# A streaming x + alpha * fx: chunks of two sizes, and three stores on ScalarE's DMA queue

## The chip, the cores and the metric

The kernel runs on one core of one Trainium2 chip. The metric is the device time of one execution in microseconds (us); lower is better. Times before: the median of 7 runs is 152.57 us, from 152.4 to 153.15.

## The reference

```python
B, S, D = 512, 32, 640
# x, fx: (B, S, D) bf16; alpha: (1,) bf16

def reference(x, fx, alpha):
    return x + alpha * fx
```

Each element is read once from x and once from fx, and written once. Each tensor has 10,485,760 elements, 20.97 MB.

## The kernel before

Each tensor is seen as 128 partitions of 81,920 consecutive elements. These are cut into five chunks of 16,384 columns (`CHUNK`), so one transfer of a chunk is 128 rows of 32 KB, 4.19 MB.

alpha is fetched once with a small DMA on ScalarE's queue and spread over the 128 partitions by a matmul with ones (`alpha_to_lanes`, L17 to L27). It is then a per-partition scalar in `a_f`.

For each chunk k there are four steps:

- `load_x(k)` (L57, DMA issued at L59) into a tile of the pool `xs`, which has four buffers
- `load_f(k)` (L61, DMA at L63) into a tile of the pool `fs`, which has two buffers
- `compute(k)` (L65, instruction at L69): one VectorE instruction, f * a_f + x, written in place over the x tile. `compute(4, 2)` does it in two halves
- `store(k)` (L78, DMA at L80) from the x tile to the output. Chunk 4 is stored in two halves

All loads and stores are issued by SyncE (`nc.sync`), thus on one DMA queue, in the order in which L85 to L105 name them, since the schedule is manual. Where an instruction needs something that isn't there yet, the tile framework lets it wait, and what stands behind it on the same engine waits too. The waits that matter here:

- `compute(k)` waits for both its loads
- `store(k)` waits for its compute
- `load_f(k)` waits for `compute(k-2)`, which read the same buffer of `fs`
- `load_x(4)` waits until `store(0)` has landed, since `xs` has four buffers

In the queue the transfers then stand as x0, f0, x1, f1, x2, f2, store 0, x3, f3, store 1, x4, f4, store 2, store 3, and the two halves of store 4.

Of the kernel before, what the change touches and what calls it, by code (L numbers as in the profile page):

```python
# [1 line left out]

# [4 lines left out]

ACT = mybir.ActivationFunctionType
ALU = mybir.AluOpType
F32 = mybir.dt.float32  # L10
BF16 = mybir.dt.bfloat16

CHUNK = 16384


def alpha_to_lanes(nc, consts, psum, alpha, eng):

    P = nc.NUM_PARTITIONS
    a_1 = consts.tile([1, 1], alpha.dtype, name="a_1")
    eng.dma_start(out=a_1[:], in_=alpha[None, :])  # L20
    ones = consts.tile([1, P], alpha.dtype, name="ones")
    nc.vector.memset(ones[:], 1.0)  # L22
    a_ps = psum.tile([P, 1], F32, name="a_ps")
    nc.tensor.matmul(a_ps[:], ones[:], a_1[:], start=True, stop=True)  # L24
    a_f = consts.tile([P, 1], F32, name="a_f")
    nc.vector.tensor_copy(out=a_f[:], in_=a_ps[:])  # L26
    return a_f  # L27


@with_exitstack  # L30
def kernel(
    ctx: ExitStack,
    tc: tile.TileContext,
    x: bass.AP,
    fx: bass.AP,
    alpha: bass.AP,
    out: bass.AP,
):
    nc = tc.nc
    P = nc.NUM_PARTITIONS  # L40
    xv = x.flatten_outer_dims().rearrange("(p n) d -> p (n d)", p=P)
    fxv = fx.flatten_outer_dims().rearrange("(p n) d -> p (n d)", p=P)
    ov = out.flatten_outer_dims().rearrange("(p n) d -> p (n d)", p=P)
    F = xv.shape[1]
    K = F // CHUNK
    assert K * CHUNK == F and K == 5

    consts = ctx.enter_context(tc.tile_pool(name="consts", bufs=1))
    psum = ctx.enter_context(tc.tile_pool(name="psum", bufs=1, space=bass.MemoryType.PSUM))
    xs = ctx.enter_context(tc.tile_pool(name="xs", bufs=4))  # L50
    fs = ctx.enter_context(tc.tile_pool(name="fs", bufs=2))
    ctx.enter_context(tc.manual_schedule())

    a_f = alpha_to_lanes(nc, consts, psum, alpha, nc.scalar)
    xt, ft = {}, {}

    def load_x(k):  # L57
        xt[k] = xs.tile([P, CHUNK], x.dtype, tag="x", name="x_t")
        nc.sync.dma_start(out=xt[k][:], in_=xv[:, bass.ts(k, CHUNK)])  # L59

    def load_f(k):  # L61
        ft[k] = fs.tile([P, CHUNK], fx.dtype, tag="f", name="f_t")
        nc.sync.dma_start(out=ft[k][:], in_=fxv[:, bass.ts(k, CHUNK)])  # L63

    def compute(k, parts=1):  # L65
        n = CHUNK // parts
        for j in range(parts):
            s = bass.ts(j, n)
            nc.vector.scalar_tensor_tensor(  # L69
                out=xt[k][:, s],  # L70
                in0=ft[k][:, s],
                scalar=a_f[:],
                in1=xt[k][:, s],
                op0=ALU.mult,
                op1=ALU.add,
            )

    def store(k, j=0, parts=1):  # L78
        n = CHUNK // parts
        nc.sync.dma_start(  # L80
            out=ov[:, k * CHUNK + j * n : k * CHUNK + (j + 1) * n],
            in_=xt[k][:, bass.ts(j, n)],
        )

    load_x(0)  # L85
    load_f(0)
    load_x(1)
    load_f(1)
    load_x(2)
    compute(0)  # L90
    load_f(2)
    store(0)
    load_x(3)
    compute(1)
    load_f(3)
    store(1)
    load_x(4)
    compute(2)
    load_f(4)
    store(2)  # L100
    compute(3)
    store(3)
    compute(4, 2)
    store(4, 0, 2)
    store(4, 1, 2)  # L105


# [1 line left out]
_INS = ['x', 'fx', 'alpha']  # L109
_OUTS = [((512, 32, 640), 'bfloat16')]  # L110


# [23 lines left out]
```

## Time and profile before

| what | value |
|---|---|
| median of 7 runs | 152.57 us |
| the profiled execution | 153.07 us |
| its span, from the first to the last instruction | 151.3 us |
| bytes read, written | 41.94 MB, 20.97 MB |
| one compute of 16,384 columns, of 8,192 | 17.29 us, 8.75 us |
| last compute begins, second half ends | 121.56 us, 138.97 us |
| first DMA issue | 0.73 us |

A profile is of one execution. Its engine rows cut the span in 40 equal slices and give the busy share of each slice in tenths. The DMA row is the mean over the core's 16 DMA engines, on which the rows of one transfer are spread, 8 rows on each. DVE is VectorE, SP is SyncE, ACT is ScalarE; SPq is SyncE's sequencer, which issues the DMAs and waits for semaphores. A wait there delays only what is issued behind it; transfers that are already in the queue go on.

### The profile page before, as it was taken

Reading aid. Unit: us, or ns where it says so; the run is one execution under the profiler, and the core shown is the slowest. Engines: PE = TensorE matmul, PEld = TensorE weight load, DVE = VectorE, ACT = ScalarE, POOL = GpSimd, SP = SyncE. Lnnn points to the kernel's source line nnn. Section 1 sums busy time; section 2 is a strip of 40 time slices with the busy share of each in tenths; the row PEclk is TensorE's granted clock in tenths of the full one; section 3 lists DMA queues with packets and bytes.
Section 4 is the critical chain, followed back from the end, with each engine's and each line's share of the span. In section 5 each row is a group of like instructions: output and inputs, shape, how many; then the busy total and the mean of one; then the engine's idle time right before and its main releaser. Section 6 shows DMA issues by size and latency. Waiting matters only on the chain.

```text
span 151.3 us, 85 instructions
## 1 busy us (share of the span) xinstructions
PE 0.2 (0%) x1; PEld 0.1 (0%) x1; DVE 86.9 (57%) x8; POOL 0.2 (0%) x4
## 2 busy tenths in 40 slices
PE   0000000000000000000000000000000000000000
PEld 0000000000000000000000000000000000000000
DVE  0000009999689997599990007999800089997000
POOL 0000000000000000000000000000000000000000
DMA  6999999999999999999999999999999999999993
GB/s 199 442 442 442 416 416 416 433 451 450 442 442 416 416 416 416 390 442 416 416 416 442 450 433 416 425 451 425 416 433 450 433 433 425 433 425 403 425 429 156
DMA packets 2306, 62.92 MB, mean 416 GB/s; under 512 B 258, under 2 KB 258, under 8 KB 258
## 3 DMA queue, kind: packets, MB, share of 16 engines
q1 hardware_dynamic: 2304, 62.92, 97.6%
q10 hardware_dynamic: 2, 0.00, 0.0%
HBM read 41.94 MB, written 20.97 MB: 416 GB/s over the span
## 4 chain that ended last, share of the span: by engine, by line
DMA 56%; DVE 29%; DVEq 6%; issue 0%; SPq 0%
DMA f_t<-in_fx_dram 56%; DVE x_t L69 29%; DVEq L131 6%; SPq L59 0%; DVEq L69 0%
## 5 line engine op out<-in xcount | busy, mean ns | idle before, releaser
L69 DVE SCALAR_TENSOR_TENSOR x_t<-f_t,a_f,x_t 128x16384 bf16<-128x16384 bf16 (+1 forms) x6 | 86.6, 14439 | 50.1 <-DMA f_t<-in_fx_dram 50.1
L26 DVE COPY a_f<-a_ps 128x1 f32<-128x1 f32 x1 | 0.2, 158 | 1.2 <-PE a_ps L24 1.2
L22 DVE MEMSET ones<- 1x128 bf16 x1 | 0.2, 165 | 0.8 <-PEq L120 0.8
L24 PE MATMUL a_ps<-a,ones 1*128 1x1 bf16 x1 | 0.2, 158 | 1.9 <-DMA a<-in_alpha_dram 1.9
L120 POOL MEMSET const-bfloat16-1.0<- 128x1 bf16 x1 | 0.1, 101 | 0.0
L120 POOL MEMSET const-uint8-127<- 128x1 uint8 x1 | 0.1, 101 | 0.0
L24 PEld LDWEIGHTS <-ones 1*128 1x128 bf16 x1 | 0.1, 100 | 1.0 <-DVE ones L22 1.0
L120 POOL MEMSET const-float32-0.0<- 128x1 f32 x1 | 0.1, 98 | 0.2 <-issue 0.2
L120 POOL MEMSET const-float32-1.0<- 128x1 f32 x1 | 0.1, 98 | 0.0
## 6 DMA issues: line engine op xcount, KB each, us to landing
x_t<-in_x_dram SPq DMA_DIRECT2D x5, 4096.0 KB, 34.9
f_t<-in_fx_dram SPq DMA_DIRECT2D x5, 4096.0 KB, 32.2
out_dram<-x_t SPq DMA_DIRECT2D x4, 4096.0 KB, 36.6
out_dram<-x_t SPq DMA_DIRECT2D x2, 2048.0 KB, 15.2
a<-in_alpha_dram ACTq DMA_DIRECT2D x1, 0.0 KB
```

What stands on the lines that cost most here:

```text
L22: nc.vector.memset(ones[:], 1.0)
L24: nc.tensor.matmul(a_ps[:], ones[:], a_1[:], start=True, stop=True)
L26: nc.vector.tensor_copy(out=a_f[:], in_=a_ps[:])
L69: nc.vector.scalar_tensor_tensor(out=xt[k][:, s], in0=ft[k][:, s], scalar=a_f[:], in1=xt[k][:, s], op0=ALU.mult, op1=ALU.add,)
L120: nc = _bacc.Bacc("TRN2", target_bir_lowering=False, num_devices=1)
L131: with _tile.TileContext(nc) as tc:
```

## The change

The chunks get two sizes: four of 8,192 columns (2.10 MB a transfer), then three of 16,384. The pools keep their number of buffers, and each buffer keeps room for 16,384 columns. `store` takes the engine that issues it. The stores of chunks 0, 1 and 2 are issued by ScalarE, those of chunks 3 to 6 by SyncE. In the loop `store(k - 3, ...)` is on ScalarE for k = 4 and 5, and on SyncE for k = 6. The last chunk is computed and stored in two halves, as before.

SyncE's order becomes x0, f0, x1, f1, x2, f2, x3, f3, x4, f4, x5, f5, store 3, x6, f6, store 4, store 5, and the two halves of store 6. ScalarE's order, behind alpha's DMA, is store 0, store 1, store 2. The waits on buffers are now `load_f(k)` on `compute(k-2)`, and x4, x5, x6 on the landing of stores 0, 1 and 2.

```diff
-CHUNK = 16384
+SIZES = [8192, 8192, 8192, 8192, 16384, 16384, 16384]
+STARTS = [sum(SIZES[:k]) for k in range(len(SIZES))]
+SLOT = max(SIZES)
...
+    def cols(k):
+        return slice(STARTS[k], STARTS[k] + SIZES[k])
+
     def load_x(k):
-        xt[k] = xs.tile([P, CHUNK], x.dtype, tag="x", name="x_t")
-        nc.sync.dma_start(out=xt[k][:], in_=xv[:, bass.ts(k, CHUNK)])
+        xt[k] = xs.tile([P, SLOT], x.dtype, tag="x", name="x_t")
+        nc.sync.dma_start(out=xt[k][:, : SIZES[k]], in_=xv[:, cols(k)])
...
-    def store(k, j=0, parts=1):
-        n = CHUNK // parts
-        nc.sync.dma_start(
-            out=ov[:, k * CHUNK + j * n : k * CHUNK + (j + 1) * n],
-            in_=xt[k][:, bass.ts(j, n)],
-        )
+    def store(k, eng=nc.sync):
+        eng.dma_start(out=ov[:, cols(k)], in_=xt[k][:, : SIZES[k]])
...
     load_x(2)
     compute(0)
     load_f(2)
-    store(0)
+    store(0, nc.scalar)
     load_x(3)
-    compute(1)
-    load_f(3)
-    store(1)
-    load_x(4)
-    compute(2)
-    load_f(4)
-    store(2)
-    compute(3)
-    store(3)
-    compute(4, 2)
-    store(4, 0, 2)
-    store(4, 1, 2)
+    for k in range(4, len(SIZES)):
+        compute(k - 3)
+        load_f(k - 1)
+        store(k - 3, nc.scalar if k < 6 else nc.sync)
+        load_x(k)
+    compute(4)
+    load_f(6)
+    store(4)
+    compute(5)
+    store(5)
+    n = SIZES[6] // 2
+    for s in (slice(0, n), slice(n, 2 * n)):
+        nc.vector.scalar_tensor_tensor(
+            out=xt[6][:, s], in0=ft[6][:, s], scalar=a_f[:], in1=xt[6][:, s], op0=ALU.mult, op1=ALU.add
+        )
+        nc.sync.dma_start(out=ov[:, STARTS[6] + s.start : STARTS[6] + s.stop], in_=xt[6][:, s])
```

`load_f` changes as `load_x` does, and `compute(k)` works on the first `SIZES[k]` columns of its tiles with one instruction.

More of the change, by code (lines that the diff above doesn't have):

```diff
@@ L44 @@
     F = xv.shape[1]
-    K = F // CHUNK
-    assert K * CHUNK == F and K == 5
+    assert sum(SIZES) == F
     consts = ctx.enter_context(tc.tile_pool(name="consts", bufs=1))
@@ L55, with compute @@
     xt, ft = {}, {}
+    def cols(k):
+        return slice(STARTS[k], STARTS[k] + SIZES[k])
     def load_x(k):
-        xt[k] = xs.tile([P, CHUNK], x.dtype, tag="x", name="x_t")
-        nc.sync.dma_start(out=xt[k][:], in_=xv[:, bass.ts(k, CHUNK)])
+        xt[k] = xs.tile([P, SLOT], x.dtype, tag="x", name="x_t")
+        nc.sync.dma_start(out=xt[k][:, : SIZES[k]], in_=xv[:, cols(k)])
     def load_f(k):
-        ft[k] = fs.tile([P, CHUNK], fx.dtype, tag="f", name="f_t")
-        nc.sync.dma_start(out=ft[k][:], in_=fxv[:, bass.ts(k, CHUNK)])
-    def compute(k, parts=1):
-        n = CHUNK // parts
[L67 to L75, printed above, removed]
-            )
-    def store(k, j=0, parts=1):
-        n = CHUNK // parts
-        nc.sync.dma_start(
-            out=ov[:, k * CHUNK + j * n : k * CHUNK + (j + 1) * n],
-            in_=xt[k][:, bass.ts(j, n)],
-        )
+        ft[k] = fs.tile([P, SLOT], fx.dtype, tag="f", name="f_t")
+        nc.sync.dma_start(out=ft[k][:, : SIZES[k]], in_=fxv[:, cols(k)])
+    def compute(k):
+        c = SIZES[k]
+        nc.vector.scalar_tensor_tensor(
+            out=xt[k][:, :c],
+            in0=ft[k][:, :c],
+            scalar=a_f[:],
+            in1=xt[k][:, :c],
+            op0=ALU.mult,
+            op1=ALU.add,
+        )
+    def store(k, eng=nc.sync):
+        eng.dma_start(out=ov[:, cols(k)], in_=xt[k][:, : SIZES[k]])
     load_x(0)
@@ L91 @@
     load_f(2)
-    store(0)
+    store(0, nc.scalar)
     load_x(3)
-    compute(1)
-    load_f(3)
-    store(1)
-    load_x(4)
-    compute(2)
-    load_f(4)
-    store(2)
-    compute(3)
-    store(3)
-    compute(4, 2)
-    store(4, 0, 2)
-    store(4, 1, 2)
+    for k in range(4, len(SIZES)):
[10 more added lines that the diff above has]
+    for s in (slice(0, n), slice(n, 2 * n)):
+        nc.vector.scalar_tensor_tensor(
+            out=xt[6][:, s], in0=ft[6][:, s], scalar=a_f[:], in1=xt[6][:, s], op0=ALU.mult, op1=ALU.add
+        )
+        nc.sync.dma_start(out=ov[:, STARTS[6] + s.start : STARTS[6] + s.stop], in_=xt[6][:, s])
 _INS = ['x', 'fx', 'alpha']
```

## The prediction

> **What bounds the kernel now.** I read the page first, then the answers of the DMA view for chosen stretches, then SyncE's own waits and the timeline. The page already decides most of it:
>
> ```profile
> span 151.3 us, 85 instructions
> PE 0.2 (0%) x1; PEld 0.1 (0%) x1; DVE 86.9 (57%) x8; POOL 0.2 (0%) x4
> ...
> DVE  0000009999689997599990007999800089997000
> ...
> DMA  6999999999999999999999999999999999999993
> ...
> DMA packets 2306, 62.92 MB, mean 416 GB/s; under 512 B 258, under 2 KB 258, under 8 KB 258
> ...
> q1 hardware_dynamic: 2304, 62.92, 97.6%
> ```
>
> The DMA row has a 9 in every slice but the first and the last: the 16 DMA engines never stand still. VectorE is idle for 43% of the span, and its idle time is all waiting for loads. Everything goes through one queue, q1 (SyncE's), first in, first out. So the time is a head, 62.92 MB at the rate that the engines can do, and a tail. Nothing else ends last. The rate comes from the DMA view of single stretches, each of these lines from another one (14 to 54 us, 54 to 64, 84 to 94, 114 to 124, and 140 to 148, in this order):
>
> ```profile
> DMA packets 592, 17.30 MB, mean 433 GB/s; under 512 B 64, under 2 KB 64, under 8 KB 64
> ...
> DMA packets 135, 3.90 MB, mean 390 GB/s; under 512 B 16, under 2 KB 16, under 8 KB 16
> ...
> DMA packets 144, 4.19 MB, mean 419 GB/s; under 512 B 16, under 2 KB 16, under 8 KB 16
> ...
> DMA packets 146, 4.26 MB, mean 426 GB/s; under 512 B 16, under 2 KB 16, under 8 KB 16
> ...
> DMA packets 229, 3.46 MB, mean 432 GB/s; under 512 B 18, under 2 KB 18, under 8 KB 18
> ```
>
> Pure loads run at 433 GB/s, pure stores of half chunks at 432. The three slow stretches are the three places where the queue goes from a load to a store (the end of f2, f3 and f4, followed by the stores of chunks 0, 1 and 2). The packets' records in the trace say it more sharply: a 32 KB row takes 1.213 us on its engine everywhere, except that rows at the ends of those three loads take up to 2.04 us. The excess over 1.213, added up and divided by 16 engines, is 0.81, 0.18 and 0.10 us. The two changes from a store to a load cost 0.01 and 0.02. The three sums shrink as the engines fall out of step: the 16 ends of a transfer lie 0.59 us apart at f2, 0.94 at f3, 1.53 at f4.
>
> The same records, counted off in the queue's order, give a duration per transfer: 9.68 us for 4.19 MB, 4.86 us for 2.10 MB. With them the span can be rebuilt: 1.74 (first packet) + 0.93 (the first rows take about 1.9 us) + 14 x 9.68 + 2 x 4.86 = 147.9, + 1.09 for the three changes + 0.99 by which the slowest engine ends after the mean + 1.19 from the last packet to the end = 151.2 of 151.3 us.
>
> Last, what the queue's issuer waits for, and the vector instruction by its shapes:
>
> ```profile
> SPq L80 <- DVE x_t L69: 55.9, 3, 28.6
> SPq L63 <- DVE x_t L69: 41.8, 3, 17.4
> SPq L63 <- DMA f_t<-in_fx_dram: 20.3, 2, 19.6
> SPq L59 <- DMA out_dram<-x_t: 11.4, 1, 11.4
> ...
> L69 DVE SCALAR_TENSOR_TENSOR x_t<-f_t,a_f,x_t 128x16384 bf16<-128x16384 bf16 x4 | 69.1, 17285 | 37.7 <-DMA f_t<-in_fx_dram 37.7
> L69 DVE SCALAR_TENSOR_TENSOR x_t<-f_t,a_f,x_t 128x8192 bf16<-128x8192 bf16 x2 | 17.4, 8748 | 12.5 <-DMA f_t<-in_fx_dram 12.5
> ```
>
> These waits are long but cost nothing, since the queue still holds transfers while SyncE waits.
>
> **The change, part by part.**
>
> *The bytes* stay: 41.94 MB read, 20.97 written. No term of the size of a microsecond can come from there.
>
> *Smaller transfers.* Before: 14 of 4.19 MB and 2 of 2.10. After: 8 and 14, that is six splits. One split costs 2 x 4.862 - 9.681 = 0.043 us by the records, so +0.26 us. The Trainium skill speaks against splitting ("DMA: Bandwidth & Descriptors", section "Anatomy of one DMA — SWDGE (gpsimd) path"): it fits 2.0 us per DMA plus the bytes at 436 GB/s, on another issuing path. By that, six more transfers would be an estimated 12 us and the sum some 12 us higher. This trace disagrees for queued transfers: the fixed part lies behind the neighbour's bytes.
>
> *Does the queue ever run dry?* Done by hand, with 4.86 us for each 2.10 MB and data from 2.7 us. Loads x0, f0 have landed at 12.4; compute 0 runs 12.9 to 21.7 (8.75 us). Then SyncE issues f2 and x3, and ScalarE issues the store of chunk 0. ScalarE has nothing else behind these waits than the next stores. The queue then still holds x2, f2, x3 and the store, 19 us of work. Compute 1 ends at 31.4 and adds f3 and store 1. x4 needs store 0 to have landed. If the two queues share by rows, that is at about 32.5, f2 lands at 41, compute 2 runs to 50, f4 and store 2 go out. x5 needs store 1 (about 42), x6 needs store 2 (about 66), f5 needs compute 3 (60.5). f6 needs compute 4: f4 lands at 75.5, two halves' worth of 17.29 puts that at 93.3. The loads ahead of f6 and the store of chunk 3 last until 109.4, so f6 is in the queue 16 us early. Store 5 (compute 5 ends at 112.6) is wanted at 128.7. f6 lands at 119.1, the halves of compute 6 end at 128.4 and 137.1, and the queue has stores 4 and 5 until 138.4 and the first half until 143.3. The thinnest cover is some 6 us, at the last store. If ScalarE's queue went wholly first or wholly last, these times move by up to three stores of 4.86 us at the front, the bytes waiting stay the same, and no gap opens. Earlier computes are thus worth nothing, and the new waits (x4, x5, x6 on stores 0, 1, 2, with everything later on SyncE behind them) cost nothing. Without that cover each would cost its whole length.
>
> The skill says in the same page, "Queues, rings and completion order", that each engine goes round-robin between queues at packet granularity. No row of this trace has two busy queues. By it the sharing above is right; the sum is the same without it.
>
> *Vector work.* 6 x 8.75 + 2 x 17.29 = 87.1 us against 86.6, wholly under the transfers. The end is as before: two halves of 8.75, two stores of 2.10 MB.
>
> *Changes between loads and stores in SyncE's queue.* The three old ones go: -1.09. Two new ones come (f5 to store 3, f6 to store 4): by the two later rows 0.18 + 0.10 = +0.28. Bounds: 0.03 (the store-to-load rows) and 1.6 (two at 0.81).
>
> *Stores beside loads.* This is the open term. Each of the three stores has 8 rows on each engine, which now lie between load rows, so 24 changes per engine from load to store and back, from about 22.7 to 42 and 51 to 66 us. Nothing in the trace shows two queues at once, so I bound one change by its nearest rows: at least 0 (store to load costs 0.01 to 0.02, and a gain below that has no row: pure loads and pure stores run at the same 433 and 432), at most 0.81 (the first change, engines in step). That is 0 to 19 us. The rows fall from 0.81 to 0.10 as the engines go out of step, and mixed rows put them out of step further, so I take half of the last, 0.05: 24 x 0.05 = +1.2 us.
>
> *Sum.* 0.26 - 1.09 + 0.28 + 1.2 = +0.65 us. Against the profiled execution, 153.07 us (its span 151.3 and 1.77 around it), 153.7. That execution is 0.5 above the median of the seven runs, 152.57, so on the median it is **153.2 us**, +0.4%.
>
> **The rivals.**
>
> *Mixing is free* (faster). For it: the change costs come from all engines turning at once, and row-by-row mixing never does that; the store-to-load rows are nearly free. Then the sum is 0.26 - 1.09 + 0.28 = -0.55, 152.0 us. If in addition the 0.99 us between mean and slowest engine shrinks, it reaches 151.0. Against: each engine still turns 24 times more. Zero change is at 0.55 / 24 = 0.023 us per turn.
>
> *Mixing is dear* (clearly slower). At the price of the last row, 0.10 each, 24 turns are 2.4 us, the sum +1.85, 154.4; at 0.18 they are 4.3 and the sum +3.8, 156.3. For it: those are the only measured rows of this kind. Against: they shrink steadily.
>
> *A dry queue* (slower): x4 to x6 wait for stores on a shared queue. It would decide only if a store took over 40 us longer than reckoned, since x6 is issued at 66 and wanted at 99.7. Each microsecond beyond would be one lost; 154 or more. Against it: the cover above.
>
> *The stores don't overlap at all*, the second queue being served only when the first is empty: then there are few turns, and 152.0 to 152.6 comes out, near no change.
>
> **How the numbers follow.** Forecast with 0.025 to 0.10 us a turn: 0.42 (152.6 to 154.4), of which 0.08 lies within 0.3%. Free mixing: 0.30, of which 0.25 faster and 0.05 same. No overlap: 0.08, nearly all same (0.07, and 0.01 faster). Dear mixing: 0.18. Dry queue: 0.02. So faster 0.26, same 0.20, slower 0.54, where 0.3% is 0.46 us, about what this measurement tells from no change. The range, 151.6 to 155.6, leaves out the far ends of free and of dear mixing, about 0.1 each. The likeliest case's own range is 152.6 to 154.4.
>
> **What would show it.** The DMA row of the changed kernel should be 9 throughout; a lower digit in the middle is the dry queue. ScalarE's queue should carry 6.3 MB. The rate of stretches with both queues busy, beside 433, gives the cost of a turn directly: 0.05 each predicts about 34 us of mixed stretches at 4% less. DVE's waits should be for loads only, and f6 should be issued near 93 us. I am wrong if the mixed stretches run at 433 or above, or far below 415.

## The result, and the profile after

The changed kernel takes 152.45 us (median of 26 runs, 152.13 to 153.01), beside 152.92 for the kernel before (61 runs, 152.37 to 154.42). The ratio is 0.9967, with a 95% interval of 0.9955 to 0.998: 0.33% faster, where +0.4% was forecast. Ratios here and below leave out executions that are more than 1.5% above the fastest of their kernel. The time lies in the range, the sign is wrong. The case that comes nearest is the first rival, free mixing (152.0), though part of that is luck, as the account further down shows.

Not only the median is lower: the slow end of the runs is lower by 1.4 us, the quick end only by 0.24. That was the first hint of what the change acts on.

The page of the changed kernel, the same rows as were shown of before:

```profile
span 150.6 us, 102 instructions
...
PE 0.2 (0%) x1; PEld 0.1 (0%) x1; DVE 87.3 (58%) x10; POOL 0.2 (0%) x4
...
DVE  0005979930498099200069999499991099997000
...
DMA  5999999999999999999999999999999999999994
...
DMA packets 3170, 62.92 MB, mean 418 GB/s; under 512 B 354, under 2 KB 354, under 8 KB 354
...
q1 hardware_dynamic: 2736, 56.62, 88.4%
q10 hardware_dynamic: 434, 6.29, 9.8%
```

The DMA row is again 9 from the second slice to the last but one: no dry queue. q10, ScalarE's queue, carries the 6.29 MB of three stores. The span is 0.7 us shorter and everything else is the same amount of work.

The DMA view of the changed kernel for 22 to 28 us, when the first store on ScalarE's queue begins to run, and for 28 to 42 us, when both queues are busy:

```profile
DMA packets 148, 2.28 MB, mean 380 GB/s; under 512 B 9, under 2 KB 9, under 8 KB 9
...
DMA packets 417, 6.05 MB, mean 432 GB/s; under 512 B 48, under 2 KB 48, under 8 KB 48
...
q10 hardware_dynamic: 208, 3.15, 52.4%
q1 hardware_dynamic: 209, 2.90, 48.4%
```

SyncE's waits and the vector instruction by its shapes:

```profile
SPq L67 <- DVE x_t L71: 52.7, 5, 17.4
SPq L67 <- DMA f_t<-in_fx_dram: 25.2, 4, 9.7
...
SPq L63 <- DMA out_dram<-x_t: 9.2, 2, 5.1
```

```profile
L71 DVE SCALAR_TENSOR_TENSOR x_t<-f_t,a_f,x_t 128x8192 bf16<-128x8192 bf16 x4 | 35.0, 8751 | 23.9 <-DMA f_t<-in_fx_dram 23.9
L71 DVE SCALAR_TENSOR_TENSOR x_t<-f_t,a_f,x_t 128x16384 bf16<-128x16384 bf16 x2 | 34.6, 17285 | 17.7 <-DMA f_t<-in_fx_dram 17.7
L104 DVE SCALAR_TENSOR_TENSOR x_t<-f_t,a_f,x_t 128x8192 bf16<-128x8192 bf16 x2 | 17.4, 8749 | 7.3 <-DMA f_t<-in_fx_dram 7.3
```

The waits are other ones and of other lengths, with VectorE's large instructions still waiting for loads alone; under a DMA row that is full none of them moves the end. In the DMA view the queues share by halves, 208 packets against 209, and the mixed stretch runs at 432 GB/s, as pure loads did before. Only the arrival of the first store is slow. By the packets' records, with the same counting as in the prediction, the excess of rows over their plain time is 0.63 us there (22 to 28 us), 0.00 from 28 to 97 us, 0.08 from 97 to 104 us and 0.09 at f6 to store 4 (about 118 us). The third of these places is not the change from f5 to store 3, which comes at about 95.4 us and costs 0.00; it is the change back, from the last rows of store 3 to x6, at about 100 us.

The last thing to look at is the end. For before and then for the changed kernel, each microsecond from 147 to 150 with the DMA share in the last column but one (the zeros are the engines' busy times; a row is booked where it starts, so shares just over 1 occur too):

```profile
147.00:148.00 1.00, 0.00 (x0) 0.00 (x0) 0.00 (x0) 0.00 (x0) 1.00 0.95 410
148.00:149.00 1.00, 0.00 (x0) 0.00 (x0) 0.00 (x0) 0.00 (x0) 1.00 0.77 328
149.00:150.00 1.00, 0.00 (x0) 0.00 (x0) 0.00 (x0) 0.00 (x0) 1.00 0.08 33
```

```profile
147.00:148.00 1.00, 0.00 (x0) 0.00 (x0) 0.00 (x0) 0.00 (x0) 1.00 0.99 426
148.00:149.00 1.00, 0.00 (x0) 0.00 (x0) 0.00 (x0) 0.00 (x0) 1.00 0.65 279
149.00:150.00 1.00, 0.00 (x0) 0.00 (x0) 0.00 (x0) 0.00 (x0) 1.00 0.00 0
```

Before has a tail in which one or two of the 16 engines still work (8% of 16 is about one engine). After, no row of data starts later than 149 us. In the records the mean engine ends at 149.12 us before and 148.94 after, 0.18 apart; the slowest ends at 150.11 and 149.40, 0.71 apart. So most of the gain in this pair of profiles, 0.53 of 0.71 us, is that the engines end closer together. The pair is further apart than the medians are, which differ by 0.47 us.

### The profile page after: what moved, and what is told of

Read it like the earlier page. It is cut to its first block, busy times and chain, and to the rows that moved or that the text cites. A ratio compares the mean times of both kernels' runs of the same rounds, so it can differ in the third digit from the quotient of the medians.

```text
span 150.6 us, 102 instructions
## 1 busy us (share of the span) xinstructions
PE 0.2 (0%) x1; PEld 0.1 (0%) x1; DVE 87.3 (58%) x10; POOL 0.2 (0%) x4
## 3 DMA queue, kind: packets, MB, share of 16 engines
q10 hardware_dynamic: 434, 6.29, 9.8%
## 4 chain that ended last, share of the span: by engine, by line
DMA 56%; DVE 29%; DVEq 6%; issue 0%; SPq 0%
DMA f_t<-in_fx_dram 56%; DVE x_t L71 23%; DVE x_t L104 6%; DVEq L133 6%; SPq L63 0%; DVEq L71 0%; DVEq L104 0%
## 5 line engine op out<-in xcount | busy, mean ns | idle before, releaser
L71 DVE SCALAR_TENSOR_TENSOR x_t<-f_t,a_f,x_t 128x8192 bf16<-128x8192 bf16 (+1 forms) x6 | 69.6, 11596 | 41.6 <-DMA f_t<-in_fx_dram 41.6
L104 DVE SCALAR_TENSOR_TENSOR x_t<-f_t,a_f,x_t 128x8192 bf16<-128x8192 bf16 x2 | 17.4, 8749 | 7.3 <-DMA f_t<-in_fx_dram 7.3
```

Source lines behind the costliest of these rows:

```text
L71: nc.vector.scalar_tensor_tensor(out=xt[k][:, :c], in0=ft[k][:, :c], scalar=a_f[:], in1=xt[k][:, :c], op0=ALU.mult, op1=ALU.add,)
L104: nc.vector.scalar_tensor_tensor(out=xt[6][:, s], in0=ft[6][:, s], scalar=a_f[:], in1=xt[6][:, s], op0=ALU.mult, op1=ALU.add)
```

## The experiments

The theories after the result. **Q**: what costs is a change from a load to a store within one queue, and taking stores out of the load queue removes such changes. **C**: the smaller first transfers bring it, since the engines start 0.29 us apart and not 0.58 (the ends of x0 in the two profiles). As experiments went on, Q was sharpened to **Q2**: each change costs some tenths of a microsecond, varying from run to run, and it doesn't matter whether a second queue or the order removes it.

**Sizes alone.** All stores back on SyncE's queue.

```diff
-    store(0, nc.scalar)
+    store(0)
...
-        store(k - 3, nc.scalar if k < 6 else nc.sync)
+        store(k - 3)
```

> The new chunk sizes, with all stores on SyncE's queue. Theory Q (the second queue brings the gain: it takes stores 0 to 2 out of the load queue, so that only the first of them costs anything): the gain is gone, since the load queue has five changes from load to store, 0.8 + 0.18 + 3 x 0.10 = 1.3 us before any step apart, and six more splits cost 0.26; ratio to before 1.000 to 1.004. Theory C (the smaller first transfers bring it: the engines start 0.29 us apart and not 0.58, and end 0.68 apart and not 1.53): ratio 0.995 to 0.998, as with the whole change.

Measured: 153.68 us, ratio 1.0064 (1.0026 to 1.0102). C falls: the new chunks alone make the kernel slower than before, and in its profile the ends of x0 lie 0.55 us apart, so the smaller transfers don't make for a close start by themselves. Q had the sign; its upper end, 1.004, lies within the interval and below the ratio. This kernel has five changes from load to store in its one queue. By the records they cost 0.84, 0.04, 0.14, 0.05 and 0.16 us in the profiled execution.

**The second queue alone.** The old five chunks, stores 0 and 1 on ScalarE.

```diff
-    def store(k, j=0, parts=1):
+    def store(k, j=0, parts=1, eng=nc.sync):
...
-        nc.sync.dma_start(
+        eng.dma_start(
...
-    store(0)
+    store(0, eng=nc.scalar)
...
-    store(1)
+    store(1, eng=nc.scalar)
```

> The old five chunks, with stores 0 and 1 on ScalarE's queue and stores 2 to 4 on SyncE's. Theory Q: two of the three changes leave the load queue, only the first store still costs 0.6 to 0.8; the excess of rows over their plain time falls from 1.09 to some 0.8 us and the ends of the engines draw together; ratio 0.995 to 0.998. Theory C: the engines still start 0.58 us apart, nothing is gained; ratio 0.999 to 1.002. The forecast's price of 0.05 per turn would give 16 turns, +0.8 us, ratio 1.003.

Measured: 152.68 us, ratio 0.9984 (0.9958 to 1.0011). The interval holds both theories' values and leaves out the forecast's price per turn. The excess at the first store is 0.94 us in its profile, and 0.09 at its only change in SyncE's queue. Inconclusive between Q and C.

**Twice the turns.** Each store on ScalarE in two transfers.

```diff
     def store(k, eng=nc.sync):
-        eng.dma_start(out=ov[:, cols(k)], in_=xt[k][:, : SIZES[k]])
+        parts = 2 if eng is nc.scalar else 1
+        n = SIZES[k] // parts
+        for j in range(parts):
+            eng.dma_start(
+                out=ov[:, STARTS[k] + j * n : STARTS[k] + (j + 1) * n],
+                in_=xt[k][:, j * n : (j + 1) * n],
+            )
```

> The changed kernel, with each of the three stores on ScalarE's queue cut into two transfers of 4096 columns, so that each engine takes 48 store rows of 8 KB between load rows and not 24 of 16 KB. Turns that are free (the trace shows no excess in any mixed stretch behind the first store): only three more splits, +0.1 us, ratio to before 0.996 to 0.999, excess in 28 to 75 us 0.00. Turns at 0.025 us each: 24 more cost 0.6, ratio 1.001; at the forecast's 0.05, 1.2 us, ratio 1.004.

Measured: 152.15 us (152.05 to 152.49), ratio 0.9942 (0.992 to 0.9965). The median is lower than even free turns had it, and the excess from 28 to 75 us is 0.04 us. Its DMA view for 28 to 42 us, for comparison with the one of the changed kernel:

```profile
DMA packets 557, 6.05 MB, mean 432 GB/s; under 512 B 64, under 2 KB 64, under 8 KB 64
...
q1 hardware_dynamic: 278, 4.03, 67.5%
q10 hardware_dynamic: 279, 2.02, 34.2%
```

The price per turn, the term that gave the forecast its sign, is zero within what can be read. The medians of this kernel and of the changed one are 0.3 us apart, but the intervals of their ratios overlap. Whether the halves themselves gain anything is not shown.

**A small first store.** The first 512 columns as a chunk of their own.

```diff
+    T = 512
...
+    nc.sync.dma_start(out=xw[:], in_=xv[:, :T])
+    nc.sync.dma_start(out=fw[:], in_=fxv[:, :T])
+    nc.vector.scalar_tensor_tensor(
+        out=xw[:], in0=fw[:], scalar=a_f[:], in1=xw[:], op0=ALU.mult, op1=ALU.add
+    )
+    nc.scalar.dma_start(out=ov[:, :T], in_=xw[:])
```

> The changed kernel with its first 512 columns as a chunk of their own, loaded first, computed and stored on ScalarE's queue within the first 10 us; chunk 0 has 7680 columns. It asks what the 0.63 us at the first store are. Theory F (a cost of the first store of the execution, whatever its size): it moves to the first microseconds, and the store of chunk 0 costs nothing; the total stays, or falls by up to 0.6 us if it falls into the time in which the first rows are slow anyway; ratio 0.993 to 0.997. Theory S (a cost of engines turning in step): the store of chunk 0 costs its 0.5 to 0.6 us again, and the small one comes on top; ratio 0.997 to 1.001.

Measured: 153.61 us, ratio 1.0041 (1.0009 to 1.0073). In the profile there is no excess from 7 to 22 us, where the small store runs, and the store of chunk 0 costs its 0.60 as ever. So F falls: the 0.6 us isn't the price of the first store of an execution whatever its size. S is not shown either, since the small one cost nothing on top. Profiled a second time:

> The kernel with the small first chunk, profiled a second time, since its first profile was of one of its quickest executions (152.62 us against a median of 153.61). Theory Q2 has no place for 1 us more: its two changes in SyncE's queue are those of the changed kernel. If this execution is again quick, nothing is learnt; if it takes 153.5 or more, the excess shows the place, and by Q2 it lies at one of the changes, by theory M (rows that begin 1 KB off) it is spread over all rows.

This execution took 153.36 us. The excess has risen from 1.56 to 1.81 us, and the rise lies before 30 us, 0.14 at the start and 0.15 at chunk 0's store; the mean engine ends 0.41 us later, and the ends are 0.94 us apart and not 0.44. There is more at the beginning, neither at SyncE's changes nor spread over all rows. Executions of 154.0 to 154.4 us, half of its runs, were not caught in a profile. Why this kernel is slower stays open.

**The changed kernel again**, with three others on one chip.

> The changed kernel once more, beside the three next ones on one chip, and a second profile of it. Ratio to before 0.995 to 0.999 as before; excess of rows over their plain time again only at the start, at the first store (about 24 us) and at the two changes in SyncE's queue (about 100 and 118 us).

Measured: 152.47 us (152.22 to 152.83), ratio 0.9968 (0.9948 to 0.9987). The excess lies at the same places: 0.71 at the first store, 0.05 from store 3 to x6, 0.04 at f6 to store 4, and again 0.00 at f5 to store 3. The expectation's "about 100 us" is thus not a change from load to store.

**One change fewer.** Store 3 on ScalarE as well.

```diff
-        store(k - 3, nc.scalar if k < 6 else nc.sync)
+        store(k - 3, nc.scalar)
```

> The changed kernel with the store of chunk 3 on ScalarE's queue too. SyncE's queue then has one change from load to store (f6 to store 4) and not two. Theory Q2 (each such change in the load queue costs some tenths of a microsecond, varying from run to run; turns between the two queues cost nothing after the first store): 0.1 to 0.4 us below the changed kernel, no excess at 100 us. Theory H (only the grain of the mixed rows matters): the same as the changed kernel within 0.1 us.

Measured: 152.25 us (152.04 to 152.46), ratio 0.9953 (0.9935 to 0.997). It is 0.22 us below the changed kernel, as Q2 had it, though the intervals overlap. There is no excess at 100 us; but there is none at 118 either, where this kernel still has its one change from load to store. So the profile doesn't show the price that Q2 puts on each change. The engines end 0.51 us apart.

**The same with halved stores.**

> The stores of chunks 0 to 3 on ScalarE's queue, each cut in two halves of 4096 columns. Theory Q2: as with four whole stores on ScalarE's queue, plus 0.1 us for the splits. Theory H: as the changed kernel with halved stores was, 152.1 to 152.2 us or a ratio of 0.994, and thus below the kernel with four whole stores.

Measured: 152.18 us (152.06 to 152.34), ratio 0.9948 (0.9926 to 0.9969). It can't be told from whole stores, so the halves' own effect (H) isn't shown. In its profile there is no excess at its one change either (0.00 at 118 us), and the engines end 0.29 us apart, the closest of all kernels. With the three halved stores it is the quickest version found, 0.5% under before.

**The order alone.** One queue, the old chunks, the same 16 transfers as before; only x3 and f3 go ahead of store 0.

```diff
     load_f(2)
-    store(0)
     load_x(3)
     compute(1)
     load_f(3)
+    store(0)
     store(1)
```

> The kernel before with only its order changed: x3 and f3 go ahead of store 0, so that SyncE's queue, still the only one, reads x0 f0 x1 f1 x2 f2 x3 f3, stores 0 and 1, x4 f4, stores 2, 3, 4. Two changes from load to store and not three, the same transfers. Theory Q2: 0.1 to 0.4 us below before (ratio 0.997 to 0.9995), with excess at about 80 and 118 us only. If it is not the count of changes but the mixing of the two queues that brings the gain: ratio 1.000, with the 0.8 us at the first store and what is left at the second as large as the two before.

Measured: 152.49 us (152.16 to 152.73), ratio 0.9955 (0.9934 to 0.9975). This is the decisive run. With no second queue, no split and no new chunk, two changes from load to store in place of three give the whole gain of the change, and more than Q2 asked for. So neither the second queue nor the chunk sizes are needed for it. The order takes away one change from store to load too (one is left of two), but in the profiles of before these cost only 0.01 to 0.03 us each. Its span, and its DMA view for 74 to 84 us, the end of f3, and then for 84 to 104 us, with the two stores and the next load:

```profile
span 150.9 us, 85 instructions
```

```profile
DMA packets 139, 4.03 MB, mean 403 GB/s; under 512 B 16, under 2 KB 16, under 8 KB 16
...
DMA packets 296, 8.65 MB, mean 433 GB/s; under 512 B 32, under 2 KB 32, under 8 KB 32
```

The first store costs its 0.83 us (by the records) at 76 to 80 us now, and not at 58 to 62: it goes where the store goes. The second change, at 118 us, costs 0.17. The profiled execution took 152.70 us, at the upper end of its runs.

**More changes.** The kernel before, with stores 0 and 1 halved and a load put between the halves.

```diff
-    store(0)
+    store(0, 0, 2)
     load_x(3)
+    store(0, 1, 2)
     compute(1)
     load_f(3)
-    store(1)
+    store(1, 0, 2)
     load_x(4)
+    store(1, 1, 2)
```

> The kernel before, one queue and the old chunks, with stores 0 and 1 cut in halves and a load put between the halves: f2, store 0a, x3, store 0b, f3, store 1a, x4, store 1b, f4, stores 2, 3, 4. Five changes from load to store and not three, two more splits (0.09 us). Theory Q2 (each change in one queue costs 0.2 to 0.5 us in the median): 0.5 to 1.1 us above before, ratio 1.003 to 1.007. If the count of changes doesn't matter: ratio 1.000 to 1.001.

Measured: 154.44 us (152.88 to 155.56), ratio 1.0075 (1.0042 to 1.0108). Its runs scatter over 2.7 us. Its span and the last microseconds, as above:

```profile
span 153.1 us, 88 instructions
```

```profile
148.00:149.00 1.00, 0.00 (x0) 0.00 (x0) 0.00 (x0) 0.00 (x0) 1.00 0.80 344
149.00:150.00 1.00, 0.00 (x0) 0.00 (x0) 0.00 (x0) 0.00 (x0) 1.00 0.20 82
150.00:151.00 1.00, 0.00 (x0) 0.00 (x0) 0.00 (x0) 0.00 (x0) 1.00 0.08 33
151.00:152.00 1.00, 0.00 (x0) 0.00 (x0) 0.00 (x0) 0.00 (x0) 1.00 0.04 16
```

Here the spread of the engines is plainest. For three microseconds a few engines still work while the others are done. The mean engine ends at 149.43 us, only 0.31 later than before; the slowest ends at 151.74, 1.63 later. In the records the ends of a transfer lie 0.68 us apart up to f1, then 0.86 at f2, 1.06, 1.95 and 3.05 at the next three changes; the last change adds nothing. The excess at the five changes is 0.88, 0.03, 0.26, 0.16 and 0.05 us, so they don't cost alike. In no profile of a single queue do the ends draw together again by more than 0.1 us: each engine has its own eight rows of every transfer, and rows of one size take the same time on all engines, so one that is behind stays behind.

**Before, a second profile.**

> The kernel before, profiled a second time, to see which of its losses come again. Theory Q2: 0.6 to 0.9 us at f2 to store 0, and at the two later changes amounts that differ from the first profile's 0.18 and 0.10; nothing between the changes.

This one took 153.46 us, a span of 151.7. The excess is 1.00 us at the first store (56 to 62), 0.08 at f3 to store 1 and 0.23 at f4 to store 2, against 0.81, 0.18 and 0.10 in the first profile; the ends are 1.66 us apart. Nothing lies between, but for 0.05 us at the two changes back to loads.

**All stores on ScalarE.**

```diff
-        store(k - 3, nc.scalar if k < 6 else nc.sync)
+        store(k - 3, nc.scalar)
...
-    store(4)
+    store(4, nc.scalar)
...
-    store(5)
+    store(5, nc.scalar)
...
-        nc.sync.dma_start(out=ov[:, STARTS[6] + s.start : STARTS[6] + s.stop], in_=xt[6][:, s])
+        nc.scalar.dma_start(out=ov[:, STARTS[6] + s.start : STARTS[6] + s.stop], in_=xt[6][:, s])
```

> The changed kernel with every store on ScalarE's queue. Free turns: mixed stretches run at 431 to 433 GB/s all the same, with no excess after the first store. But stores 4 and 5 now share the engines with x6 and f6 and don't stand behind them: f6 lands near 138 us and not 120, the last half of compute ends near 156, and the queues run dry before the last store; span near 163 us.

Measured: one execution, 165.5 us. Its span, its DMA row, the rate of 28 to 52 us, and VectorE's last instructions from the timeline (start, duration, engine, line):

```profile
span 163.7 us, 101 instructions
...
DMA  5999999999999999999999899998999998007466
```

```profile
28.00:52.00 24.00, 0.00 (x0) 0.00 (x0) 12.38 (x2) 0.00 (x0) 1.00 1.02 435
```

```profile
139.13 17.41 DVE L104 SCALAR_TENSOR_TENSOR x_t<-f_t,a_f,x_t 128x8192 bf16<-128x8192 bf16 x2 [20.60 <-DMA f_t<-in_fx_dram]
```

The stretch runs at 435 GB/s, so turns are free here too, and yet 13 us are lost, since stores 4 and 5 take about half of the engines' time from x6 and f6. The last compute begins at 139.13 and not at 120.79, and the two zeros in the DMA row are the dry queue. It shows what the prediction's cover was worth, and why the late stores belong behind the late loads.

## Why the prediction was wrong, by its own steps

**Right.** The bound: DMA busy throughout, no dry queue. The hand-made schedule: computes foreseen at 12.9, 76 and 95.3 us began at 12.98, 76.75 and 96.19; f6 was issued at 94.06 (93.3), x6 at 67.23 (66). One sum in it is off without harm: x6 issued at 66 and wanted at 99.7 leaves a cover of 34 us, and not over 40. Sharing by rows: 208 and 209 packets, and in the records the rows of the two queues alternate on each engine. The splits' +0.26 us is not shown by itself in any run; three more splits (halved stores) came out no slower.

**Mis-sized: the stores beside loads.** This is the largest miss of the sum. It took 24 turns at 0.05 us, +1.2. Measured are 0.63 us at the first store and 0.00 at all other turns; with 48 turns in place of 24 it is 0.04 in all behind the first store. The prediction had named the sign of this error itself, mixed stretches at 433 GB/s or above: 28 to 42 us ran at 432, 30 to 70 us at 434. The row that the price came from, the last change in the old queue, was read as a price of turning. But what it shows doesn't recur when rows of two queues alternate.

**Mis-taken for a constant: the spread of the engines.** The prediction put 0.99 us between the mean and the slowest engine into its rebuilt span and let it stand, mentioning that it might shrink only in a rival. It became 0.46. That is 0.53 of the 1.35 us between the forecast sum (+0.65) and the profiles' difference (-0.7). The mixing term gives 0.57, the new changes in SyncE's queue 0.11 (0.17 and not 0.28), the start 0.09 (0.69 and not 0.78 of excess); together 1.30. Part of the spread's 0.53 was there from the start: at the landing of x0 the slowest engine was 0.32 us behind the mean before and 0.14 after. Over the profiles this start is 0.14 to 0.31 us where the first transfers are small and 0.22 to 0.34 where they are large. The ranges overlap, and no run separates what the smaller chunks add to it. The spread was visible in the trace of before: the prediction itself lists 0.59, 0.94 and 1.53 us at f2, f3 and f4, and used the numbers only to argue that the price falls.

**Mis-placed: the changes in SyncE's queue.** The 0.28 us stood for f5 to store 3 and f6 to store 4. The first cost 0.00, the second 0.09, and 0.08 came where the prediction put nothing, from store 3 back to x6.

**Luck in the rival.** Free mixing, at -0.55 us, is near the measured -0.7, but its terms are not what happened. It took the first store's price as gone, and that was paid again (0.63). With the measured terms its sum is 0.26 - 1.09 + 0.17 + 0.63 = -0.03, no change. What made the kernel quicker in this pair of profiles is the spread and the start, which stand in no sum of the prediction.

**What the runs put in place of these steps.** Counting changes from load to store where one queue holds everything: two give 0.9955 (order alone), three are before, five give 1.0064 (sizes alone) and 1.0075 (more changes). The intervals of fewer and of more than three lie on either side of 1, the order-alone run has the same 16 transfers, and more changes adds two splits (0.09 us by the prediction's rows). This much is shown: within one queue, fewer changes are quicker and more are slower.

For kernels with two queues the count doesn't order the runs. Two changes in SyncE's queue give 0.9967 and 0.9968, with halved stores 0.9942; one gives 0.9953 and 0.9948, but 0.9984 with the old chunks (its interval reaches 0.9958); the one with the small first chunk has two and is slower, 1.0041, its losses at the beginning. Nor is there a price per change: in the profiles the changes behind the first large store cost from 0.00 (f5 to store 3 in the changed kernel, f6 to store 4 with four stores on ScalarE) to 0.26 us. That the change gains because it takes three stores out of the load queue thus fits the one-queue runs, but is argued, and not shown by itself.

Two more things remain open: what the loss at a change is made of, and why the first large store costs 0.5 to 1.0 us in every kernel, on either queue and at 24 as at 78 us, when a store of 1 KB rows before it costs nothing.

## What to carry to other kernels

In a kernel bound by DMA, rebuild the span per engine, not only in the mean: the slowest of 16 sets the end, and within one queue it didn't catch up here. Group loads and stores so that a single queue turns from one to the other seldom (two changes against three were worth 0.45%), or try early stores on the other queue, where turning cost nothing behind the first store; keep the late stores behind the late loads. Where runs scatter, look for what scatters them before pricing a change from one profile.

## What the runs showed of the hardware

With both queues busy, an engine took rows from them in turn whatever their length: rows of 8, 16 and 32 KB next to each other took their plain time (0.309, 0.611 and 1.213 us), and from 30 to 70 us the changed kernel and that with halved stores both moved 434 GB/s, where one queue moved 433. The first row of a store on ScalarE's queue ran 4.4 us after the issue when the engines were busy with loads (issue 21.76, first row 26.14 us; for the third store 48.5 and 52.88), and nearly all the slow load rows of the first store lay in the 2.5 us before its first row; before the third store there were none. And a reordering of the same 16 transfers in one queue was worth 0.45%, 0.25 to 0.66% by its interval.
